# Attention times v in tiles of 128 rows by 32 columns, the row sums right behind it, and a copy split over two engines

## The chip, the cores and the metric

The kernel runs on one core of a Trainium2 chip. The metric is the device time of one execution in microseconds (us); the kernel before takes 552.08 us, the median of three runs (551.88 to 552.08). Of the core's engines the text names TensorE (PE in the profile's rows, PEld for its weight loads), VectorE (DVE), ScalarE (ACT), GpSimd (POOL) and SyncE (SP), whose queue issues nearly all DMAs. TensorE writes into PSUM, which here is used as four pairs of banks, PS[0] to PS[3].

## The reference

Three layers follow each other, on 4 batches of 576 positions: attention with rotated q and k, 8 heads of 64 channels; a gated layer with a layer norm and a product over positions; a layer with a short convolution as gate. The change lies in the first:

```python
q_rot, k_rot = rotate(q), rotate(k)
scores = (1 / sqrt(D)) * q_rot @ k_rot^T          # 576 x 576 for each head
scores = scores - max(scores, axis=-1)
attn = exp(scores)
attn = attn / (sum(attn, axis=-1) + 1e-09)
out = attn @ v                                    # then the two other layers
```

All arithmetic is fp32 in its accuracy: products with q and k are made of high and low parts in a reduced format, the product with v and the row sums are fp32 matmuls. An fp32 matmul shows as two MATMUL instructions with a weight load each.

## The kernel before, in words

Heads are taken in pairs: 16 pairs, two heads side by side in the 128 partitions. For each pair the loop in `attention` (L805 to 824) calls `phase`, which puts two things on TensorE in a fixed, hand-written order of units: the exponent scores of pair i (nine units `t` and `T`, L662 and L670, each followed by an exponential on ScalarE, L675, that leaves keys on partitions and query positions on columns in nine tiles `e`) and the plain scores of pair i + 1 (`y`, `x` and `S`, L610 and L620), of which VectorE takes row maxima out of PSUM (L613, L622), because the exponential needs each row's maximum ahead. For the pairs 1 to 14 the order begins `y t y t t x t ...`; in the last phase there are no maxima. Which pair of banks each unit takes follows from a small model of when the banks come free: in the phases after the first, the first `y` takes PS[0], the first `t` PS[1], the second `y` PS[2], the second `t` PS[3], and the third `t` takes PS[0] again, which it may write when the first maximum is done.

Behind each phase stands what the text calls the product stage. `pv_unit` (L689 on) multiplies the exponentials with v: four units of two key blocks each, for 512 of the 576 keys, into PS[3]: the weights are 64 channels of v for 128 keys, the moving data 288 query positions, and the two halves of the positions go to the partitions 0 to 63 and 64 to 127 (L699). Two such matmuls stand beside each other in the array. A fifth call with `(8,)` adds the remaining 64 keys of both heads with tiles of 64 rows by 64 columns (L709) and copies PS[3] to the tile `xu` on ScalarE (L713, through the helper at L263), from where two DMAs on SP's queue store it (L717). Then `sum_unit` (L722 on) adds the exponentials over the keys by matmuls with ones: tiles of 128 rows by 32 columns, four beside each other, into PS[2] (L733). ScalarE copies the sums (`ss`, L737), a DMA spreads them (`rc`), VectorE takes reciprocals in `sum_end` (L745), and a DMA stores these.

GpSimd has added a part of the exponentials before (tiles `ac`), and in six of the pairs it adds more, so that the sums take 24 MATMULs instead of 32.

During the product stage VectorE and ScalarE prepare pair i + 2: four elementwise operations that rotate q and k (`prep_high`, L259), casts on ScalarE (`qp`, `qh`, `kh`), and, in the pairs 1 to 8, the conversion of a weight tile (`wa_half`, L309 to L315); in the pairs 9 to 13 VectorE makes the low part of k instead (`kl`).

The order of the instructions on each engine is set once by a planner (`Plan.order`). Every operation is added with a cost in us. TensorE's operations keep the order in which they are added; on the other engines, whenever an engine is free in the planner's own time, the operation that is ready and has the earliest due time goes next, where due times are counted back from the end along the dependences (an engine may also be held for a more urgent operation that comes soon). The costs decide only this order; on the chip each engine runs its list and waits on semaphores.

Of the kernel before, what the change touches and what calls it, by code (L numbers as in the profile page):

```python
# [21 lines left out]
B, HP, S, DM, HALF = 4, 4, 576, 512, 288  # L22
# [120 lines left out]
def dve(n):  # L143
    return 0.08 + n / 960
# [20 lines left out]
FP32 = 0.48  # L165
# [5 lines left out]
def mixer_kernel(ctx: ExitStack, tc: tile.TileContext, qk, v, vrem, cs, w_in, g_ln, w_sgT, b_sg,  # L171
                 w_out, w_val, conv_w, w_out2, out):
    nc = tc.nc
# [3 lines left out]
    add = P.add  # L177
# [14 lines left out]
    xu_d = [dram.tile([HP, 128, S], F32, name=f"xu_d{b}") for b in range(B)]  # L192
# [69 lines left out]
    def acopy(out_, in_, n, r, w, after=()):  # L262
        return add("Act", act(n), lambda: nc.scalar.copy(out_(), in_()), r, w, after)  # L263
# [384 lines left out]
    EU = {}  # L648
# [40 lines left out]
    def pv_unit(i, us):  # L689

        j2 = i % 2
        pv, kp = PS[3], ("ps", 3)
        if us[0] < 8:
            j = UNITS[us[0]][0]

            def mm():
                for h in range(2):
                    for hf in range(2):
                        nc.tensor.matmul(pv[64 * hf:64 * hf + 64, h, 0:HALF], VM[j2][:, j, h], E[EU[i, us[hf]]][:, h],  # L699
                                         start=j == 0, stop=False, skip_group_check=True)  # L700
            add("PE", 2 * FP32 + (0.2 if not j else 0.0), mm, [*[("e", EU[i, u]) for u in us], ("vm", j2)], [kp])
            return
        e = E[EU[i, 8]]

        def mm():
            for hf in range(2):
                for h in range(2):
                    rows = slice(64 * h, 64 * h + 64)
                    nc.tensor.matmul(pv[64 * hf:64 * hf + 64, h, 0:HALF], VR[j2][rows], e[rows, hf], start=False, stop=True,  # L709
                                     skip_group_check=True)  # L710
        add("PE", FP32 + 0.1, mm, [("e", EU[i, 8]), ("vr", j2)], [kp])
        xu = XU[j2]
        acopy(lambda: xu, lambda: pv[:, :, 0:HALF], S, [kp], [("xu", j2)])  # L713

        def st(q):
            for hf in range(2):
                q.dma_start(out=xu_d[i // HP][i % HP, :, HALF * hf:HALF * hf + HALF].rearrange("(h d) c -> d h c", h=2),  # L717
                            in_=xu[64 * hf:64 * hf + 64])
        dma(290, st, [("xu", j2)], [("xu_d", i)], n=2)

    def sum_unit(i, ps, kps):

        j2 = i % 2
        src = [(ones, ones, [(E[EU[i, u + hf]], h) for h in range(2) for hf in range(2)], ("e", EU[i, u]),
                ("e", EU[i, u + 1])) for u in (4, 6)[adds(i) // 2 - 1:]]
        src.append((ones, ones, [(AC[hf], h) for h in range(2) for hf in range(2)], ("ac", 0), ("ac", 1)))
        e = EU[i, 8]
        src.append((*ones_b, [(E[e], hf) for h in range(2) for hf in range(2)], ("e", e)))

        def mm():  # L730
            for n, x in enumerate(src):
                for t, (a, y) in enumerate(x[2]):
                    nc.tensor.matmul(ps[32 * t:32 * t + 32, 0, 0:HALF], x[t // 2], a[:, y], start=n == 0,  # L733
                                     stop=n == len(src) - 1, skip_group_check=True)
        add("PE", len(src) * FP32 + 0.15, mm, [*[k for x in src for k in x[3:]], ("consts",)], [kps])
        ss, rc = SS[0], RC[j2]
        add("Act", act(HALF), lambda: nc.scalar.activation(ss, ps[:, 0, 0:HALF], AF.Copy, bias=1e-9), [kps], [("ss", 0)])  # L737

        def rows(q):
            q.dma_start(out=rc, in_=ss[0:97:32].rearrange("t (p c) -> t p c", c=9))  # L740
        dma(5, rows, [("ss", 0)], [("rc", j2)])
# [22 lines left out]
    def attention():  # L764
        keep_busy(16)
        first_pairs()

        def phase(i, vl):

            order = "ytyttxtttyttyxTS" if i + 1 < NPAIR else "ttttttttT"  # L770
            if not i:
                order = "xtttyttytyttyxTS"
            free = [0.0, 0.0, 0.74 if i else 0.0, 0.0]
            pe, ac, dv = 0.2, 0.0, 0.0
            nt, xs, ys = 0, iter(range(2)), iter(range(2, 6))
            for x, what in enumerate(order):
                ks = range(4) if x < len(order) - 4 else range(3)
                at_once = [k for k in ks if free[k] <= pe]
                k = max(at_once, key=lambda k: free[k]) if at_once else min(ks, key=lambda k: free[k])
                pe = max(pe, free[k])  # L780
                if what in "tT":
                    pe += 4 * PASS if what == "t" else 8 * PASS + 0.24
                    act_at = max(ac, pe + 0.22)
                    ac, free[k] = act_at + 0.55, act_at + 0.75
                    st_unit(i, nt, PS[k], ("ps", k))
                    add_unit(i, nt)
                    nt += 1
                else:
                    pe += 2 * PASS if what == "S" else MAXIMA[what == "y"][0]
                    dve_at = max(dv, pe + 0.29)  # L790
                    dv = dve_at + (0.67 if what == "S" else MAXIMA[what == "y"][1])
                    free[k] = dv + 0.15
                    s_unit(i + 1, {"x": xs, "y": ys, "S": iter((8,))}[what].__next__(), PS[k], ("ps", k))
                if not x:
                    first = [P.last_pe, *vl]
                    if 2 <= i + 1 < NPAIR:
                        prep_low(i + 1, first)
                if x == (12 if i < FOUR else 0):
                    job_s(i, [P.last_pe])
            if i + 1 < NPAIR:  # L800
                s_end(i + 1)

        vl = []
        for i in range(NPAIR):
            if i + 2 < NPAIR:  # L805
                prep_load(i + 2)
            if i and i + 1 < NPAIR:
                load_v(i + 1)
            if i:
                job_loads(i)  # L810
            phase(i, vl)
            ep.append(P.last_pe)
            rot = [P.last_pe]
            if 0 < i < FOUR or i == NPAIR - 1:
                sum_end(i - 1, [*rot, *P.writer.get(("mn", (i + 1) % 2, 1), ())] if i + 1 < NPAIR else ())
            if i + 2 < NPAIR:
                rot = prep_high(i + 2, [P.last_pe, *P.writer[("mn", (i + 1) % 2, 1)]])
            vl = job_v(i, [P.last_pe], rot)
            if FOUR <= i < NPAIR - 1:
                sum_end(i - 1, P.writer["kl", (i + 1) % 3])  # L820
            for us in ((0, 2), (1, 3), (4, 5), (6, 7), (8,)):
                pv_unit(i, us)
            sum_unit(i, PS[2], ("ps", 2))
        sum_end(NPAIR - 1)

    def unit(cost, mm, r, new=True):
# [414 lines left out]
```

## Time and profile before

| | |
|---|---|
| median of three runs | 552.08 us |
| the profiled execution | 552.56 us, its span 550.8 us |
| TensorE, its weight loads | 541.4 us busy (98%), 463.3 (84%) |
| VectorE | 411.7 us busy (75%) |
| ScalarE | 278.4 us busy (51%) |
| GpSimd | 247.5 us busy (45%) |
| granted TensorE clock | 0.998 of full speed |

The span runs from the first instruction to the last. Busy times are from a trace of one execution; matmuls are pipelined, so that one that is shown with 0.41 us can be followed by the next after much less, and their ends are modelled. The chain of work that ended last is followed back from the last instruction, at each step to what released it. Idle time of an engine that nothing waits for costs nothing.

### The profile page before, as it was taken

What the parts mean: (1) busy time and instruction counts of PE and PEld (TensorE: products, weight loads), DVE (VectorE), ACT (ScalarE), POOL (GpSimd) and SP (SyncE); (2) the same over time, 40 slices, a digit from 0 to 9 for tenths busy, and PEclk for the clock granted to TensorE, in tenths of its full rate; (3) what the DMA queues carried; (4) which work ended last, traced back from release to release, by engine and by line L of the source; (5) the groups of instructions that cost most, each with busy time, mean ns of one, the idle gap of its engine ahead of it and who ended that gap; (6) DMA issues with size and microseconds to landing.
All of it is one profiled execution on the core that took longest, in us unless ns stands there. A gap on an engine that the chain in (4) does not pass through costs nothing.

```text
span 550.8 us, 11758 instructions
## 1 busy us (share of the span) xinstructions
PE 541.4 (98%) x4592; PEld 463.3 (84%) x4592; DVE 411.7 (75%) x595; ACT 278.4 (51%) x451; POOL 247.5 (45%) x229
## 2 busy tenths in 40 slices
PE   6999999999999999999999999999999999999996
PEld 5877777777777777679989989989999998899985
DVE  7878888888888888969768556654979997649610
ACT  3567766776666667635526136134157543334221
POOL 5545555555555555456967677554610011222000
PEclk9999999999999999999999999999999999999999
DMA  5565656565666664774484762643264211110022
GB/s 187 141 195 142 184 152 175 160 185 153 188 171 160 168 198 103 214 223 111 131 295 119 231 189 75 196 142 124 104 208 128 73 44 72 44 58 1 0 77 96
DMA packets 58024, 77.39 MB, mean 141 GB/s; under 512 B 29392, under 2 KB 34000, under 8 KB 57968
## 3 DMA queue, kind: packets, MB, share of 16 engines
q1 hardware_dynamic: 57664, 76.37, 46.8%
q8 instruction: 36, 0.59, 0.4%
q10 hardware_dynamic: 304, 0.26, 0.1%
q14 instruction: 20, 0.16, 0.1%
HBM read 55.94 MB, written 18.95 MB: 136 GB/s over the span
## 4 chain that ended last, share of the span: by engine, by line
PE 96%; DVE 2%; DMA 1%; ACT 0%; issue 0%; SPq 0%; ACTq 0%; DVEq 0%
PE ps L840 55%; PE ps L662 12%; PE ps L699 12%; PE ps L733 6%; PE ps L670 4%; PE ps L610 4%; PE ps L709 2%; PE ps L951 2%; DVE raw L259 1%; DVE mx L613 1%; DMA raw<-qk 1%; PE ps L620 1%; DVE mn L622 0%; ACT ob L263 0%; ACT kh L263 0%
## 5 line engine op out<-in xcount | busy, mean ns | idle before, releaser
L613 DVE TENSOR_REDUCE mx<-ps 128x2 f32<-128x640 f32 (+1 forms) x96 | 89.1, 957 | 28.8 <-PE ps L610 21.9
L675 ACT ACTIVATE e<-ps 128x576 f32<-128x576 f32 x144 | 87.0, 652 | 20.3 <-PE ps L670 10.9
L699 PE MATMUL ps<-e,vm 128*64 128x288 f32 x512 | 65.6, 409 | 0.0
L699 PEld LDWEIGHTS ps<-e,vm 128*64 128x64 f32 x512 | 35.3, 137 | 24.7 <-issue 2.6
L260 POOL TENSOR_TENSOR ac<-e,e 128x576 f32<-128x576 f32 x32 | 45.2, 1431 | 9.4 <-ACT e L675 9.4
L840 PE MATMUL ps<-s_h,vn 128*128 128x288 f32 x256 | 46.9, 295 | 0.0
L259 DVE TENSOR_TENSOR raw<-raw,cst 128x1152 f32<-128x1152 f32 (+1 forms) x33 | 42.0, 1272 | 0.5 <-DMA raw<-qk 0.5
L263 ACT CAST qp<-raw 128x512 fp32r<-128x512 f32 x16 | 18.6, 1164 | 45.2 <-DVE raw L259 45.2
L840 PEld LDWEIGHTS ps<-s_h,vn 128*128 128x128 f32 x256 | 38.3, 188 | 0.0
L662 PE MATMUL ps<-qh,kh 64*128 64x288 f32 x256 | 38.3, 295 | 0.0
L662 PE MATMUL ps<-qh,kl 64*128 64x288 f32 x256 | 37.9, 292 | 0.0
L662 PE MATMUL ps<-ql,kh 64*128 64x288 f32 x256 | 37.8, 292 | 0.0
L662 PE MATMUL ps<-mr,one_r 64*128 64x288 f32 x256 | 37.7, 290 | 0.0
L260 POOL TENSOR_TENSOR vs<-vs,u 128x576 f32<-128x576 f32 x16 | 27.0, 1688 | 19.3 <-DVE vs L955 16.8
L610 PE MATMUL ps<-kh,qp 64*128 64x320 f32 (+1 forms) x256 | 32.7, 312 | 2.3 <-ACT kh L263 2.2
L1032 DVE SCALAR_TENSOR_TENSOR gt<-xm,cw,gt 128x576 f32<-128x576 f32 x32 | 28.9, 909 | 1.8 <-ACT gt L1029 1.4
L610 PEld LDWEIGHTS ps<-kh,qp 64*128 64x128 f32 x256 | 21.7, 184 | 10.0 <-ACT kh L263 7.7
L309 DVE TENSOR_SCALAR wt<-wt 128x256 f32<-128x256 f32 (+1 forms) x28 | 16.4, 586 | 16.5 <-ACT wt L319 16.5
L260 POOL TENSOR_TENSOR xl<-xs,xh 128x576 fp32r<-128x576 f32 x2 | 5.3, 2633 | 50.0 <-ACT xh L263 50.0
L840 PE MATMUL ps<-XL,w_h 128*128 128x288 f32 x128 | 27.4, 296 | 0.0
L840 PE MATMUL ps<-XH,w_l 128*128 128x288 f32 x128 | 27.4, 295 | 0.0
L840 PE MATMUL ps<-XH,w_h 128*128 128x288 f32 x128 | 27.4, 295 | 0.0
(181 smaller groups left out, 1493.4 us busy)
## 6 DMA issues: line engine op xcount, KB each, us to landing
raw<-qk SPq DMA_DIRECT2D x31, 576.0 KB
xu_d<-xu SPq DMA_DIRECT2D x32, 144.0 KB
rb<-r_d SPq DMA_DIRECT2D x32, 144.0 KB
xs<-xu_d SPq DMA_DIRECT2D x16, 288.0 KB
x_d<-xs SPq DMA_DIRECT2D x16, 288.0 KB
g_d<-vs SPq DMA_DIRECT2D x16, 288.0 KB
vm<-v SPq DMA_DIRECT2D x16, 256.0 KB
wr<-w_in SPq DMA_DIRECT2D x8, 512.0 KB
```

Of the source, the lines that this page charges most:

```text
L259: return add("DVE", dve(n), lambda: nc.vector.tensor_tensor(out_(), a(), b(), op), r, w, after, lock=True)
L260: return add("Pool", pool(n), lambda: nc.gpsimd.tensor_tensor(out_(), a(), b(), op), r, w, after, lock=True)
L263: return add("Act", act(n), lambda: nc.scalar.copy(out_(), in_()), r, w, after)
L610: nc.tensor.matmul(ps[:, h, w * y:w * y + w], QP[j2][rows, c], kh[rows, keys], start=True, stop=True)
L613: add("DVE", MAXIMA[n // 2 > 0][1], lambda: nc.vector.tensor_reduce(out=MX[j2][:, n // 2 > 0, :, chunks[0]:chunks[-1] + 1], in_=ps[:, :, 0 ...
L662: nc.tensor.matmul(ps[:, h, 0:HALF], x[rows, keys] if o < 3 else x[rows], y[rows, cols], start=o == 0, stop=o == 3)
L670: nc.tensor.matmul(ps[:, hf, 0:HALF], x, y[:, cols], start=o == 0, stop=o == 3)
L675: add("Act", 0.62, lambda: nc.scalar.activation(E[n], ps[:, :, 0:HALF], AF.Exp), [kps], [("e", n)])
L699: nc.tensor.matmul(pv[64 * hf:64 * hf + 64, h, 0:HALF], VM[j2][:, j, h], E[EU[i, us[hf]]][:, h], start=j == 0, stop=False, skip_group_chec ...
L733: nc.tensor.matmul(ps[32 * t:32 * t + 32, 0, 0:HALF], x[t // 2], a[:, y], start=n == 0, stop=n == len(src) - 1, skip_group_check=True)
L840: nc.tensor.matmul(out_(y), lhs(p, k, y), rhs(q, k, y), start=not z, stop=ends and z == len(terms) - 1)
L1032: add("DVE", dve(S) + 0.05, lambda dd=dd, m=m, x2=x2, gt=gt: nc.vector.scalar_tensor_tensor(gt(), x2()[:, m:m + S], cw[:, 5 * dd + m:5 * d ...
```

## The change

In `pv_unit` each product of two key blocks is cut into four tiles of 128 rows by 32 columns instead of two of 128 by 64: the tile `t` takes 32 of the 64 channels (`t % 2`) for one half of the positions (`t // 2`), so there are twice as many matmuls and weight loads of half the width. In `attention` the row sums are issued behind the four units of the product, and the remainder `(8,)` last. The copy of PS[3], which follows the remainder, is split: head 0 on ScalarE, head 1 on VectorE, each 128x288 elements, and the two stores wait for both. Some of the planner's costs change with it.

```diff
             def mm():
                 for h in range(2):
-                    for hf in range(2):
-                        nc.tensor.matmul(pv[64 * hf:64 * hf + 64, h, 0:HALF], VM[j2][:, j, h], E[EU[i, us[hf]]][:, h],
-                                         start=j == 0, stop=False, skip_group_check=True)
-            add("PE", 2 * FP32 + (0.2 if not j else 0.0), mm, [*[("e", EU[i, u]) for u in us], ("vm", j2)], [kp])
+                    for t in range(4):
+                        nc.tensor.matmul(pv[32 * t:32 * t + 32, h, 0:HALF], VM[j2][:, j, h, 32 * (t % 2):32 * (t % 2) + 32],
+                                         E[EU[i, us[t // 2]]][:, h], start=j == 0, stop=False, skip_group_check=True)
+            add("PE", 2 * FP32 + (0.1 if not j else 0.0), mm, [*[("e", EU[i, u]) for u in us], ("vm", j2)], [kp])
             return
...
-        acopy(lambda: xu, lambda: pv[:, :, 0:HALF], S, [kp], [("xu", j2)])
+        acopy(lambda: xu[:, 0], lambda: pv[:, 0, 0:HALF], HALF, [kp], [("xu", j2, 0)])
+        add("DVE", dve(HALF), lambda: nc.vector.tensor_copy(xu[:, 1], pv[:, 1, 0:HALF]), [kp], [("xu", j2, 1)])
...
-        dma(290, st, [("xu", j2)], [("xu_d", i)], n=2)
+        dma(290, st, [("xu", j2, h) for h in range(2)], [("xu_d", i)], n=2)
...
-        add("PE", len(src) * FP32 + 0.15, mm, [*[k for x in src for k in x[3:]], ("consts",)], [kps])
+        add("PE", len(src) * FP32, mm, [*[k for x in src for k in x[3:]], ("consts",)], [kps])
...
-            for us in ((0, 2), (1, 3), (4, 5), (6, 7), (8,)):
+            for us in ((0, 2), (1, 3), (4, 5), (6, 7)):
                 pv_unit(i, us)
             sum_unit(i, PS[2], ("ps", 2))
+            pv_unit(i, (8,))
```

## Rows read from the trace of the kernel before

**Rows 1.** The page: busy us of each engine, and the chain by engine.

```profile
PE 541.4 (98%) x4592; PEld 463.3 (84%) x4592; DVE 411.7 (75%) x595; ACT 278.4 (51%) x451; POOL 247.5 (45%) x229
...
PE 96%; DVE 2%; DMA 1%; ACT 0%; issue 0%; SPq 0%; ACTq 0%; DVEq 0%
```

**Rows 2.** Stretches (start:end): length, busy us by engine, clock, DMA share, GB/s.

```profile
26.00:236.50 210.50, 210.37 (x2438) 152.18 (x2437) 179.96 (x250) 142.32 (x233) 109.40 (x93) 1.00 0.61 170
236.50:546.00 309.50, 309.50 (x1939) 292.56 (x1936) 211.28 (x320) 122.84 (x200) 122.76 (x95) 1.00 0.38 118
```

**Rows 3.** Chain, pair 7: start us, us, engine, tile, line, instructions.

```profile
122.98 4.03 PE ps L699 x32
127.01 0.65 PE ps L709 x8
127.66 2.08 PE ps L733 x32
```

**Rows 4.** Chain, pair 9, where the sums are shorter.

```profile
155.33 1.59 PE ps L733 x24
```

**Rows 5.** TensorE's timeline, pair 7: start, us, line, out<-in, shapes; first row cut at 125.0.

```profile
122.91 2.40 PE L699 MATMUL ps<-e,vm 128*64 128x288 f32 x18
...
122.91 4.10 PE L699 MATMUL ps<-e,vm 128*64 128x288 f32 x32
126.94 0.71 PE L709 MATMUL ps<-e,vr 64*64 64x288 f32 x8
...
129.67 0.41 PE L610 MATMUL ps<-kh,qp 64*128 64x320 f32 x2
```

**Rows 6.** ScalarE's timeline, pair 7, the copy and the cast behind it.

```profile
127.91 0.63 ACT L263 COPY xu<-ps 128x576 f32<-128x576 f32 x1
128.45 0.67 ACT L263 CAST kh<-raw 128x576 fp32r<-128x576 f32 x1
```

**Rows 7.** Timeline, pair 14: the remainder and the copy that follows it.

```profile
221.70 0.72 PE L709 MATMUL ps<-e,vr 64*64 64x288 f32 x8
...
222.48 0.64 ACT L263 COPY xu<-ps 128x576 f32<-128x576 f32 x1 [0.85 <-DMA krl<-kl]
```

**Rows 8.** VectorE's timeline at the end of pair 7's product stage; in brackets its idle time.

```profile
129.32 0.43 DVE L315 SCALAR_TENSOR_TENSOR wf<-wr,wt 128x256 int32<-128x256 int32 x1
129.66 0.21 DVE L745 RECIPROCAL rc<-rc 128x9 f32<-128x9 f32 x1
130.12 0.83 DVE L613 TENSOR_REDUCE mx<-ps 128x2 f32<-128x640 f32 x1 [0.25 <-PE ps L610]
```

**Rows 9.** TensorE's weight loads, first of the third exponent unit behind pair 7.

```profile
131.00 0.19 PEld L662 LDWEIGHTS ps<-qh,kh 64*128 64x128 f32 x2
```

**Rows 10.** Timeline, pair 13: a maximum, and a weight load that waited for it.

```profile
202.75 0.83 DVE L613 TENSOR_REDUCE mx<-ps 128x2 f32<-128x640 f32 x1 [0.80 <-PE ps L610]
...
203.63 0.19 PEld L620 LDWEIGHTS ps<-kh,qr 128*128 128x128 f32 x1
```

**Rows 11.** VectorE by line and form: busy us, mean ns; the rows of 288 elements.

```profile
L259 DVE TENSOR_TENSOR raw<-raw 128x288 f32<-128x288 f32 x4 | 1.8, 458 | 0.1
```

**Rows 12.** VectorE's timeline at the end of pair 8's product stage.

```profile
143.21 0.42 DVE L315 SCALAR_TENSOR_TENSOR wf<-wr,wt 128x256 int32<-128x256 int32 x1
143.96 1.58 DVE L613 TENSOR_REDUCE mx<-ps 128x2 f32<-128x640 f32 x2 [0.32 <-PE ps L610]
```

**Rows 13.** VectorE's timeline, pair 11, and where TensorE starts the next scores.

```profile
181.88 0.76 DVE L259 TENSOR_TENSOR raw<-raw 128x576 f32<-128x576 f32 x1
...
183.23 0.21 DVE L745 RECIPROCAL rc<-rc 128x9 f32<-128x9 f32 x1
184.00 0.83 DVE L613 TENSOR_REDUCE mx<-ps 128x2 f32<-128x640 f32 x1 [0.56 <-PE ps L610]
...
183.54 0.42 PE L610 MATMUL ps<-kh,qp 64*128 64x320 f32 x2
```

**Rows 14.** SP's queue, pair 7: the stores of the copy.

```profile
134.07 2.22 SPq L717 DMA_DIRECT2D xu_d<-xu  x2
```

## The prediction

> **What bounds the kernel now.** I read the page first: TensorE is busy 98% of the span and holds 96% of the chain that ended last [rows 1], where VectorE has 2%. The view of stretches says the same of attention (26.0 to 236.5 us) and of all that follows: 210.4 of 210.5 us and 309.5 of 309.5 us, at full clock [rows 2]. The whole change lies in attention, and behind it TensorE never idles; so each microsecond that TensorE's order loses or gains there moves the end by as much, and what another engine does counts only where it makes TensorE wait. The order on TensorE is the order of the program: the scores and exponentials of a pair of heads, then a product stage, and so 16 times.
>
> The chain shows that stage in its parts: 4.03 us for the 32 matmuls with v, 0.65 for the 8 of the remainder, 2.08 for the 32 of the row sums, 6.75 together [rows 3]; in six of the pairs the sums are only 24 matmuls, 1.59 us [rows 4]. The timeline gives the pace inside: from 18 to 32 matmuls with v the end moves by 4.10 - 2.40 = 1.70 us, seven groups of two, 0.243 us a group [rows 5]. The sums go in groups of four tiles of 32 columns, and eight fewer of them save 2.08 - 1.59 = 0.49 us, again 0.243 to 0.245 a group. So a group of four narrow tiles costs what two wide ones do, and each part pays something for the entry into and the exit from its tile shape: 4.03 - 16 x 0.243 = 0.14 us for the product with v, 0.65 - 2 x 0.243 = 0.16 for the remainder, 2.08 - 8 x 0.243 = 0.14 for the sums.
>
> **Part 1: tiles of 32 columns, sums right behind, remainder last.** 64 matmuls in 16 groups of four, then the 8 groups of the sums in the same shape, one entry and one exit: 24 x 0.243 + 0.14 = 5.97, and 0.65 for the remainder: 6.62 instead of 6.75 (6.13 instead of 6.27 where the sums are shorter). One shape change of 0.14 us goes, 16 x 0.14 = 2.2 us. The entry from the full array into narrow tiles is not in the trace (before, they are entered from the remainder). The two other changes bound it: if the new entry costs up to 0.03 more the sum is 1.8, if it costs less it is 2.4; I take 2.2, the sums' own row. The 512 added matmuls and weight loads I cost at nothing: loads run beside matmuls, 152 of the 210 us of attention against 210 of matmuls [rows 2], and the sums keep 0.243 with as many loads.
>
> The Trainium skill speaks against this part: by "TensorEngine Tiling (Array Packing)", section Instruction Overhead, each matmul carries about 60 cycles of its own, so one should not buy tiles with more instructions; 512 x 60 cycles at 2.4 GHz are 12.8 us, an estimate from that page alone. It is a rival below.
>
> **Part 2: the copy moves behind the stage's end and half of it goes to VectorE.** The old copy, 0.63 us on ScalarE, stood between the casts of q and k, 1.8 us ahead of the next scores [rows 5, 6]. Now the accumulator (the fourth pair of banks) is complete only with the remainder's last matmul. In an undisturbed place (at 222 us) the copy began 0.06 us after the remainder's modelled end [rows 7], and that end, 126.94 + 0.71, lies 0.06 behind the stage's end. So both halves can start 0.12 us after the next scores have begun.
>
> ScalarE is free there: the copy of the sums, done earlier now, is out of the way, and the next exponential needs a finished unit of new scores first. VectorE is not. Call R the start of its first maximum (L613) of the next scores before the change, 0.45 us into them (130.12 to 129.67) [rows 5, 8]. TensorE waits on this instruction without slack: the third unit of exponent scores reuses its banks, and its first weight load started at 131.00, while the maximum ended at 130.95 [rows 8, 9]; VectorE's end reaches TensorE's load 0.05 us later (203.58 to 203.63) [rows 10]. So whatever delays the first maximum delays TensorE by the same, and it isn't made up for.
>
> Price of the half copy: no row has it. The nearest is the addition of 128x288 elements, 0.458 us [rows 11]; from above the maximum over 640 elements out of PSUM, 0.83 [rows 10]; from below the reciprocal of 9, 0.21 [rows 8]. An independent successor starts some 0.08 before such an end (129.66 after 129.32 + 0.43) [rows 8]. I take 0.458 - 0.08 = 0.38 us, the row of the same width; the ends are 0.13 and 0.75. VectorE keeps its order, so the first maximum stands behind the copy: the copy can begin first, and its banks are needed first, by the second unit of exponent scores.
>
> New times, all by R; with 0.14 saved the scores start at R - 0.59, the copy can start at R - 0.47, the maximum's matmuls are ready at R - 0.14:
> - Pairs 1, 3, 5, 7: weight conversions and a reciprocal hold VectorE till 129.66 + 0.13 = R - 0.33 [rows 8]. The maximum starts at R - 0.33 + 0.38 = R + 0.05.
> - Pairs 2, 4, 6, 8: the reciprocal is earlier; L315 starts at 143.21 and frees VectorE 0.34 later, R - 0.41 [rows 12]. The maximum: R - 0.03.
> - Pairs 0 and 9 to 13: VectorE is free by R - 0.64 (183.23 + 0.13 against 184.00) [rows 13]. The maximum: R - 0.47 + 0.38 = R - 0.09.
> - Pairs 14 and 15: no maxima follow, and the fourth bank pair is wanted late: the full 0.14.
>
> Sum: 4 x 0.05 - 4 x 0.03 - 6 x 0.09 - 2 x 0.14 = -0.74 us. So of 2.2 us some 1.5 is given back as waits for L613.
>
> The rows thus put 0.38 us on the engine that TensorE waits for next; the 0.63 us of the whole copy on ScalarE would touch no maximum. By the Trainium skill, "TensorEngine Tiling (Array Packing)", section PSUM Bottleneck, ScalarE and VectorE should share the evacuation; by that rule alone the split is free and the sum -2.2.
>
> What else moves: in pairs 9 to 12 the cast of k, freed of the copy ahead of it, follows the addition's end at 182.64 and ends 0.03 + 0.67 later, at 183.34, 0.06 ahead of the new start at 183.54 - 0.14 = 183.40 [rows 6, 13]: just hidden; if not, it costs what it ends later, some 0.05 in four pairs. The stores of the copy went out at 134.07, 5.5 us after the copy's end [rows 6, 14]; 1.8 us later they still find it done, and on SP's queue behind them wait weight loads for later pairs; the copy of the sums and its reciprocal chain come 0.8 us earlier. Without that cover a later transfer would slip by 1.8 us, none of it read for the next two pairs.
>
> Forecast: the profiled execution took 552.56 us (span 550.8 and 1.8 around it), so 551.8 for it; it stands 0.5 above the median of the three runs, 552.08, for which I say 551.3.
>
> **Rivals.**
> - The copy is hidden, full gain. If it occupies VectorE for 0.13 us as the reciprocal does, the maximum is ready at R - 0.20 or earlier and R - 0.14 rules: 552.1 - 2.2 = 549.8. For it: VectorE idles 0.25 to 0.56 us just there [rows 8, 12, 13]. Against: the four rows of 288 elements take 0.458 [rows 11].
> - Slower: VectorE's queue at the start of the scores. The order on it is planned with costs below the rows (0.35 us for L315, whose row has 0.43 [rows 8]), so one more operation may come between the stage's end and the first maximum. Another conversion there (0.34) in eight pairs costs 2.7: 551.3 + 2.7 = 554.0. Gain and loss balance where the maximum is ready 0.16 us late by its own matmuls, as a mean over 14 pairs (2.2 / 14); the forecast has 1.5 / 14 = 0.11; from 0.24 it is slower by over 0.2%. Against: the planner gives the copy and the maximum earlier due times than conversions.
> - The change doesn't do what it says: the exit price of the wide tiles turns up at the entry of the narrow ones or of the scores. Then only the loss is left: 552.1 + 1.5 = 553.6. Against: the parts' extras are alike (0.14, 0.16, 0.14) whatever comes before and after.
> - An added matmul pays its own slot. Matmuls and loads of the sums go at 0.243 / 8 = 0.03 us each; 512 x 0.03 = 15 us, 567. Against: the sums keep 0.243 a group with the same eight instructions.
>
> **How the numbers follow.** Forecast 0.50, with its own range 550.8 to 551.9; full gain 0.20; slower by VectorE's queue 0.13; no gain from the shapes 0.08; own slots 0.02; the rest (0.07) for a new order elsewhere, to either side. 0.2%, 1.1 us, is about what a measurement of this kernel can tell from no change: faster means below 551.0, slower above 553.2. Faster: the full gain, the lower tenth of the forecast's and part of the rest, 0.34. Slower: most of the queue's and of the lost gain, 0.16. Same: 0.50. The range 549.7 to 553.6 takes in the full gain and the lost gain; the upper price of the copy, 0.75 (0.37 more in 14 pairs, 5.2 us, 556.5), stays out with most of the queue's.
>
> **What would show it.** Right: product with v and sums in one piece of about 5.97 us (5.5 with short sums), the remainder 0.65 behind it; a VectorE copy of some 0.46 us ahead of the first L613; the gap from the start of the scores to the first maximum 0.50 to 0.65 us instead of 0.45; the third unit's first load later than 1.33 us into the scores by the same. Wrong: that gap still 0.45 (then the full gain), the maximum ahead of the copy, groups slower than 0.243 us, or a different extra where the shape changes.

## The result, and the profile after

The changed kernel took 555.25 us in the median of four runs (554.31 to 555.75) against 552.08 before; the ratio is 1.0056, 95% interval 1.0038 to 1.0073. I had said 551.3 (549.7 to 553.6): the change is slower where I had forecast no change, and outside the range. The profiled execution is the fastest of the four, 554.31 us with a span of 552.5; a second one, taken with the experiments, took 555.48 with a span of 553.69.

The page of the changed kernel, busy time and the chain by engine:

```profile
PE 542.4 (98%) x5104; PEld 461.5 (84%) x5104; DVE 415.8 (75%) x611; ACT 277.3 (50%) x451; POOL 245.7 (44%) x229
...
PE 82%; DVE 8%; DMA 4%; ACT 3%; issue 2%; SPq 0%; ACTq 0%; DVEq 0%
```

The view of its stretches, from the first product stage to the end of attention and from there to the end:

```profile
25.50:238.24 212.74, 211.17 (x2950) 150.29 (x2949) 182.75 (x264) 141.13 (x232) 107.91 (x93) 1.00 0.60 166
238.24:548.00 309.76, 309.76 (x1940) 292.58 (x1936) 213.18 (x322) 122.94 (x199) 121.81 (x96) 1.00 0.37 119
```

In [rows 1] TensorE held 96% of the chain that ended last; now it holds 82%, and VectorE, ScalarE and DMAs have pieces of it. In [rows 2] TensorE was idle for 0.13 us of attention; now it is for 1.57 of 212.74. (The busy time hides more: matmuls that are followed late are shown longer.) Most of the time is lost in attention, by waits.

TensorE's timeline in pair 7 of the changed kernel, in start, us, line, out<-in and shapes:

```profile
123.64 4.09 PE L699 MATMUL ps<-e,vm 128*32 128x288 f32 x64
127.55 1.15 PE L734 MATMUL ps<-e,ones 128*32 128x288 f32 x16
...
129.60 0.72 PE L709 MATMUL ps<-e,vr 64*64 64x288 f32 x8
130.25 0.42 PE L610 MATMUL ps<-kh,qp 64*128 64x320 f32 x2
```

Product and sums run as one piece, 129.60 - 123.64 = 5.96 us, the remainder takes 0.65, and the stage 6.60 in place of 6.75 [rows 3, 5]. The gain of the tiles is there. What follows it in the same pair is not as forecast. ScalarE, VectorE and TensorE's weight loads, the same kernel, start of the next scores (130.25):

```profile
129.79 0.41 ACT L738 ACTIVATE ss<-ps 128x288 f32<-128x288 f32 x1
130.93 0.40 ACT L263 COPY xu<-ps 128x288 f32<-128x288 f32 x1 [0.73 <-DVE xu L714]
...
130.03 0.43 DVE L315 SCALAR_TENSOR_TENSOR wf<-wr,wt 128x256 int32<-128x256 int32 x1
130.38 0.21 DVE L746 RECIPROCAL rc<-rc 128x9 f32<-128x9 f32 x1
130.50 0.40 DVE L714 COPY xu<-ps 128x288 f32<-128x288 f32 x1
130.81 1.55 DVE L613 TENSOR_REDUCE mx<-ps 128x2 f32<-128x640 f32 x2
...
131.38 0.19 PEld L662 LDWEIGHTS ps<-qh,kh 64*128 64x128 f32 x2 [0.29 <-ACT xu L263]
...
131.89 0.19 PEld L662 LDWEIGHTS ps<-qh,kh 64*128 64x128 f32 x2
```

VectorE copies its half at 130.50 and starts the first maximum 0.56 us into the scores, where it was 0.45 [rows 8]: that is my forecast. But ScalarE begins its half only when VectorE's is done (the bracket: idle for 0.73 us, released by VectorE's `xu`), 0.68 into the scores. PS[3] comes free at 1.08, and the second exponent unit loads its first weights at 131.38, 1.13 in, after a wait for ScalarE's `xu`. The third unit follows 1.64 in; in [rows 9] it was 1.33.

Two other places lose time. The first is pairs 9 and 11. GpSimd's timeline at the product stage of pair 9, then VectorE's, in the kernel before:

```profile
156.69 0.17 POOL L267 COPY mark<-kl 1x1 f32<-1x1 f32 x1 [5.10 <-DVE kl L259]
156.83 0.79 POOL L260 TENSOR_TENSOR s_l<-xs,s_h 128x288 fp32r<-128x288 f32 x1
...
151.75 1.35 DVE L259 TENSOR_TENSOR raw<-raw,cst 128x1152 f32<-128x1152 f32 x1
```

and the same in the changed kernel:

```profile
152.60 0.82 POOL L260 TENSOR_TENSOR s_l<-xs,s_h 128x288 fp32r<-128x288 f32 x1
...
152.82 1.82 DVE L259 TENSOR_TENSOR raw<-raw,cst 128x1152 f32<-128x1152 f32 x1
```

The planner has put GpSimd's subtraction (`s_l`) 5 us earlier in the stage, beside VectorE's first multiply, which takes 1.82 us instead of 1.35. In pair 11 it is another subtraction (`w_l`, 0.73 us), and the multiply takes 1.72. Over all fourteen traces (before, after, e1 to e12) ten such multiplies run beside a GpSimd subtraction for 0.42 to 0.61 us; they take 1.64 to 1.82 us, each longer than 1.35 by its overlap less 0.13. The 396 others, none beside GpSimd for more than 0.12 us, take 1.29 to 1.36. All that hangs on the multiply (the rotation, the cast of k, the next scores) comes as much later, and ScalarE, by the same new plan, copies the sums ahead of that cast. The stage takes 6.68 us where pairs 10 and 12 have 6.12 and 6.13.

The second is behind the last pair. VectorE, SP's queue, GpSimd and TensorE's weight loads in the second profile of the changed kernel, whose attention ended at 238.44:

```profile
241.89 0.29 DVE L311 TENSOR_SCALAR wt<-wt 128x256 int32<-128x256 int32 x1
242.10 0.45 DVE L714 COPY xu<-ps 128x288 f32<-128x288 f32 x1
...
240.25 0.62 SPq L741 DMA_DIRECT2D rc<-ss  x1
242.58 1.28 SPq L718 DMA_DIRECT2D xu_d<-xu  x2
243.96 0.55 SPq L849 DMA_DIRECT2D xs<-xu_d  x1
244.55 0.45 SPq L322 DMA_DIRECT2D wr<-w_in  x1
...
254.55 1.27 POOL L260 TENSOR_TENSOR w_l<-wf,w_h 128x512 fp32r<-128x512 f32 x1 [5.16 <-ACT w_h L263]
...
255.87 0.30 PEld L842 LDWEIGHTS ps<-XH,w_l 128*128 128x128 f32 x2 [0.79 <-POOL w_l L260]
```

and SP's queue and GpSimd in the kernel before, whose attention ended at 236.48:

```profile
236.60 1.27 SPq L717 DMA_DIRECT2D xu_d<-xu  x2
239.29 0.43 SPq L322 DMA_DIRECT2D wr<-w_in  x1
...
250.79 1.29 POOL L260 TENSOR_TENSOR w_l<-wf,w_h 128x512 fp32r<-128x512 f32 x1 [3.33 <-ACT w_h L263]
```

VectorE's half of pair 15 stands in its queue behind weight conversions (one of them, beside a GpSimd subtraction, takes 1.47 us where it takes 0.43 alone) and ends at 242.55. The store goes out 6.0 us later than before, and the load of the next weights, behind it on SP's queue, 5.3 us later (counted from the end of attention, 4.0 and 3.3). The low part of these weights, `w_l`, is ready at 255.82, and TensorE, which wants it at 255.1, waits. In the first profile the same chain was 1.2 to 1.6 us earlier (load at 242.98) and nothing waited. That is the 1 us by which the two profiles differ behind attention; the other runs have no trace.

The lengths below are worked out from the starts of TensorE's matmuls: the product stage of pairs 0 to 8 (before: 6.75), the same of pair 9, the median of the 14 stretches of scores, the stretch from the first product stage to the end of attention, and from there to the end of the span. Each ratio is over all runs, to runs of the kernel before taken beside them (medians 552.06 to 552.13); it is not the quotient of the medians, least so in e2 and e7, whose runs are spread.

```
kernel                  stage  pair 9  scores  attention  behind it  time    ratio [95%]
before                  6.754  6.27    7.08    210.50     314.29     552.08
changed                 6.603  6.68    7.41    212.72     314.26     555.25  1.0056 [1.0038, 1.0073]
e1  changed again       6.603  6.68    7.41    212.75     315.25     555.17  1.0056 [1.0044, 1.0069]
e2  halves parallel     6.603  6.68    7.18    210.02     318.01     553.31  1.0035 [1.0017, 1.0052]
e3  one copy, ScalarE   6.604  6.14    7.10    208.74     315.76     551.70  0.9994 [0.9985, 1.0003]
e4  planner's table     6.607  6.45    7.39    213.57     314.27     554.96  1.0052 [1.0039, 1.0064]
e5  narrow tiles only   6.741  6.26    7.09    210.70     314.26     552.04  1.0001 [0.9993, 1.0010]
e6  one copy, order     6.603  6.15    7.10    209.03     314.28     550.85  0.9974 [0.9963, 0.9984]
    of before kept
e7  cast of k first     6.603  6.59    7.41    212.47     314.89     555.43  1.0076 [1.0055, 1.0098]
e8  split, old place    6.754  6.27    7.16    211.06     314.27     552.71  1.0009 [1.0000, 1.0017]
e9  split, order kept   6.603  6.13    7.54    214.49     314.56     556.41  1.0076 [1.0064, 1.0088]
e10 e9, parallel        6.603  6.14    7.18    209.28     315.99     551.84  0.9992 [0.9982, 1.0001]
e11 remainder last only 6.754  6.27    7.11    210.66     314.28     552.21  1.0003 [0.9995, 1.0012]
e12 last two pairs old  6.603  6.68    7.41    212.99     314.26     554.83  1.0052 [1.0037, 1.0066]
```

The span of the second profile is 2.92 us longer than before, and that divides so: start 0.30 less; the product stages of pairs 0 to 14 but 9 and 11, 2.12 less (0.2 of it a stall that the kernel before had in pair 13); the stages of pairs 9 and 11 0.82 more; 12 stretches of scores 3.72 more (the two behind pairs 9 and 11 are unchanged, since their late start hides the copies); the last pair 0.17 less; behind attention 0.96 more.

### The profile page after: what moved, and what is told of

It is laid out like the page before. It is cut to its first block, busy times and chain, and to the rows that moved or that the text cites. A ratio compares the mean times of both kernels' runs of the same rounds, so it can differ in the third digit from the quotient of the medians.

```text
span 552.5 us, 12851 instructions
## 1 busy us (share of the span) xinstructions
PE 542.4 (98%) x5104; PEld 461.5 (84%) x5104; DVE 415.8 (75%) x611; ACT 277.3 (50%) x451; POOL 245.7 (44%) x229
## 4 chain that ended last, share of the span: by engine, by line
PE 82%; DVE 8%; DMA 4%; ACT 3%; issue 2%; SPq 0%; ACTq 0%; DVEq 0%
PE ps L842 55%; PE ps L662 10%; PE ps L699 7%; DVE raw L259 4%; DMA raw<-qk 3%; PE ps L734 3%; DVE mx L613 2%; PE ps L670 2%; ACT e L675 2%; PE ps L610 2%; PE ps L953 2%; PE ps L709 1%; ACT xu L263 1%; DMA wr<-w_in 1%; DVE xu L714 0%
## 5 line engine op out<-in xcount | busy, mean ns | idle before, releaser
L613 DVE TENSOR_REDUCE mx<-ps 128x2 f32<-128x640 f32 (+1 forms) x96 | 88.7, 954 | 24.9 <-PE ps L610 17.5
L699 PE MATMUL ps<-e,vm 128*32 128x288 f32 x1024 | 65.4, 408 | 0.0
L699 PEld LDWEIGHTS ps<-e,vm 128*32 128x32 f32 x1024 | 31.6, 110 | 27.8 <-issue 2.6
L662 PEld LDWEIGHTS ps<-qh,kh 64*128 64x128 f32 x256 | 24.0, 184 | 4.3 <-ACT xu L263 3.5
L842 PE MATMUL ps<-s_l,vn 128*128 128x288 f32 x128 | 27.3, 294 | 0.0
```

The source lines that it names most:

```text
L613: add("DVE", MAXIMA[n // 2 > 0][1], lambda: nc.vector.tensor_reduce(out=MX[j2][:, n // 2 > 0, :, chunks[0]:chunks[-1] + 1], in_=ps[:, :, 0 ...
L662: nc.tensor.matmul(ps[:, h, 0:HALF], x[rows, keys] if o < 3 else x[rows], y[rows, cols], start=o == 0, stop=o == 3)
L699: nc.tensor.matmul(pv[32 * t:32 * t + 32, h, 0:HALF], VM[j2][:, j, h, 32 * (t % 2):32 * (t % 2) + 32], E[EU[i, us[t // 2]]][:, h], start=j ...
L842: nc.tensor.matmul(out_(y), lhs(p, k, y), rhs(q, k, y), start=not z, stop=ends and z == len(terms) - 1)
```

## Experiments

Theory A: the two halves run one after the other, and the second exponent unit waits for PS[3]. Rival B, my own forecast's term: VectorE's half delays the first maximum, and that is the cost. C: in pairs 9 and 11 the loss is ScalarE's new order, the sums ahead of the cast of k; its rival: VectorE's longer multiply. (The expectation of e3 calls another rival C.) D: what saves time is one change of tile shape fewer.

**e1, the changed kernel again** (no edit).

> The changed kernel once more, for its spread and a second profile. Expected: 554.3 to 555.8 us, 1.005 of before; in the attention's phases the second exponent unit again starts about 1.13 us after the end of the product stage, and in pairs 9 and 11 the next scores again start 0.56 us late. If the about 1 us by which its other runs lie above the profiled one is a phase wait that comes and goes, the second profile shows it in other pairs.

555.17 us; the waits in the scores are the same to 0.02 us. The variable part is behind attention (315.25 against 314.26), not in the phases as I had guessed.

**e2, the halves in parallel.** Each half reads a bank of its own; the kernel's dependences are kept per tile, and PS[3] is one tile. The edit takes back the dependence between the two readers; the next writer of PS[3] still waits for both.

```diff
-        acopy(lambda: xu[:, 0], lambda: pv[:, 0, 0:HALF], HALF, [kp], [("xu", j2, 0)])
-        add("DVE", dve(HALF), lambda: nc.vector.tensor_copy(xu[:, 1], pv[:, 1, 0:HALF]), [kp], [("xu", j2, 1)])
+        both = []
+        def half(h):
+            both.append((nc.vector.tensor_copy if h else nc.scalar.copy)(xu[:, h], pv[:, h, 0:HALF]))
+            if len(both) == 2:
+                tc.declare_no_dep(both[1].ins, both[0].ins, reason="two readers of two banks")
+        add("Act", act(HALF), lambda: half(0), [kp], [("xu", j2, 0)])
+        add("DVE", dve(HALF), lambda: half(1), [kp], [("xu", j2, 1)])
```

> The changed kernel with one thing else: the two half copies of PS[3] no longer wait for each other (they read two banks). Every engine's order is the same. Theory A (the halves ran one after the other, so PS[3] came free at 1.09 us after the product stage and not at 0.65, and the second exponent unit waits for it): both halves start 0.2 after the product, the unit starts at 0.93 again, 12 phases win back about 0.33 us each: 555.25 - 4.0 = 551.2 us (550.7 to 551.8), ratio about 0.999. Rival B (my prediction's term: VectorE's half delays the first reduction and that costs): VectorE does the same work at the same place, so 555 us as the change, ratio 1.005.

ScalarE, VectorE and the weight loads in pair 7, scores from 128.78:

```profile
128.92 0.40 ACT L716 COPY xu<-ps 128x288 f32<-128x288 f32 x1 [0.19 <-PE ps L709]
...
129.04 0.40 DVE L716 COPY xu<-ps 128x288 f32<-128x288 f32 x1
129.36 1.55 DVE L613 TENSOR_REDUCE mx<-ps 128x2 f32<-128x640 f32 x2
...
129.56 0.21 PEld L662 LDWEIGHTS ps<-qh,kh 64*128 64x128 f32 x2
...
130.23 0.18 PEld L662 LDWEIGHTS ps<-qh,kh 64*128 64x128 f32 x2
```

Both halves take 0.40 us side by side; PS[3] is free at 0.66, the second unit loads at 0.78 (129.56) without a wait, and the scores fall from 7.41 to 7.18. What remains is B: the first maximum at 0.58 and the third unit's load at 1.45 (130.23) in place of 1.33. So A costs 0.23 us a stretch and B 0.08 to 0.10; 12 stretches: 2.7 and 1.0. The Trainium skill ("PSUM — Partial Sum Buffer", section PSUM bank collisions raise a hardware error) says that two engines may not read one bank and quadrant at once, but may read different banks; the two lengths of 0.40 agree with the second half, and no run here shows the first. The time, 553.31 (551.98 to 556.74), is neither A's 551.2 nor B's 555: attention, 0.48 us shorter than before, promises 551.6. The profiled run took 555.48, and its view of stretches shows where it lost that; the other runs have no trace:

```profile
252.00:256.00 4.00, 2.15 (x11) 1.92 (x12) 3.45 (x12) 1.46 (x3) 2.69 (x4) 0.90 0.83 220
256.00:260.00 4.00, 4.00 (x24) 4.00 (x23) 3.17 (x6) 3.13 (x6) 3.67 (x5) 0.68 0.07 15
260.00:264.00 4.00, 4.00 (x33) 4.00 (x33) 3.86 (x7) 1.68 (x3) 2.56 (x3) 1.00 0.00 0
```

Attention ends 2.8 us earlier than in e1, but GpSimd starts on `w_l` only 1.2 us earlier (253.31 against 254.55); TensorE's weight loads wait for `w_h` (1.5 us) and `w_l` (0.8), and the granted clock is 0.68 in the 4 us that follow: part of them at the lower of the two levels, 1.2 GHz.

**e3, the whole copy on ScalarE.**

```diff
-        acopy(lambda: xu[:, 0], lambda: pv[:, 0, 0:HALF], HALF, [kp], [("xu", j2, 0)])
-        add("DVE", dve(HALF), lambda: nc.vector.tensor_copy(xu[:, 1], pv[:, 1, 0:HALF]), [kp], [("xu", j2, 1)])
+        acopy(lambda: xu, lambda: pv[:, :, 0:HALF], S, [kp], [("xu", j2, h) for h in range(2)])
```

> The changed kernel with the whole copy (128x576) on ScalarE alone, so the new tiles and the remainder last without the split. Theory A: the copy takes 0.63 us from about 0.2 after the product stage, PS[3] is free at 0.83, the second exponent unit's turn is at 0.93: no wait left, and ScalarE's order at pairs 9 and 11 is that of before: 555.25 - 4.0 - 1.1 = 550.1 us (549.5 to 551), ratio 0.9965. Rival C (a single copy behind the product is too late as well, the unit waits up to 0.1 to 0.2 us in each phase): 551.7 to 553.

Pair 7, scores from 128.37:

```profile
128.51 0.64 ACT L263 COPY xu<-ps 128x576 f32<-128x576 f32 x1 [0.18 <-PE ps L709]
...
128.83 1.58 DVE L613 TENSOR_REDUCE mx<-ps 128x2 f32<-128x640 f32 x2
...
129.20 0.19 PEld L662 LDWEIGHTS ps<-qh,kh 64*128 64x128 f32 x2
...
129.71 0.19 PEld L662 LDWEIGHTS ps<-qh,kh 64*128 64x128 f32 x2
```

One copy of 0.64 us ends 0.78 into the scores, and the second unit loads at 0.83; first maximum and third unit are where they were before (0.46 and 1.34). The scores are 7.10 but for two stretches of 7.47, behind pairs 6 and 12, whose cause I have not found. Attention is 1.8 us shorter than before. The time is not (551.70): 1.5 us are lost behind attention, where TensorE waits 0.9 us for GpSimd (`t`) and 0.4 for ScalarE (`gl`).

**e4, the planner's table of the banks.**

```diff
-            free = [0.0, 0.0, 0.74 if i else 0.0, 0.0]
+            free = [0.0, 0.0, 0.1 if i else 0.0, 1.1 if i else 0.0]
```

> The changed kernel with the planner's table of when the banks come free set to where the change puts them (bank pair 2 at 0.1, bank pair 3 at 1.1 us): the second exponent unit takes another bank pair, and the two halves stay one after the other. Theory A: the late release of PS[3] is hidden, 555.25 - 4.0 - 1.1 (ScalarE's order at pairs 9 and 11 also goes back) = 550.1 us (549.5 to 551). Rival B (VectorE's half and its queue cost by themselves): 554 us, only the 1.1 of pairs 9 and 11 comes back.

A miss, and it decides nothing between A and B: in pair 7 the second exponent unit still waits for ScalarE's `xu`, since four units come in a row and there are four pairs of banks. In pairs 9 to 13 the first unit, now in PS[2], waited for the copy of the sums (stage 6.45).

**e5, the narrow tiles alone**, in the kernel before: L699 as in the change, all else as it was.

> The kernel before with the product's tiles alone changed: 128 rows by 32 columns, 64 matmuls in place of 32; the remainder stays ahead of the sums, the copy is whole and on ScalarE. The product stage then has as many changes of tile shape as before (128x32, 64x64, 128x32). Theory D (a change of shape costs some 0.15 us, a narrower tile and the doubled number of matmuls nothing): 552.1 us, ratio 0.9995 to 1.0005, product stage 6.75 us. Rival (each added matmul has a cost that only the saved change of shape hid): the stage is longer by up to 32 x 10 ns = 0.3 us, 16 pairs: up to 557 us, ratio above 1.002.

Stage 6.741, 552.04 us. 64 matmuls of 32 columns take what 32 of 64 columns took (the 10 ns a matmul of the rival were a guess, from no row); TensorE's timeline, pair 7 of e5, against [rows 5]:

```profile
122.25 4.09 PE L699 MATMUL ps<-e,vm 128*32 128x288 f32 x64
126.27 0.72 PE L709 MATMUL ps<-e,vr 64*64 64x288 f32 x8
```

**e6, one copy, order of before kept.** As e3, but pairs 14 and 15 in the old form, with the old costs for the planner.

```diff
+            late = i < 14
-            for us in ((0, 2), (1, 3), (4, 5), (6, 7)):
+            for us in ((0, 2), (1, 3), (4, 5), (6, 7), *[(8,)][late:]):
                 pv_unit(i, us)
             sum_unit(i, PS[2], ("ps", 2))
-            pv_unit(i, (8,))
+            if late:
+                pv_unit(i, (8,))
```

> As the whole copy on ScalarE alone with the new tiles and the remainder last, but pairs 14 and 15 keep the order of before (remainder ahead of the sums) and the planner's costs of before, so that the order of every engine after the attention is that of the kernel before. Theory (the attention gains about 1.6 to 2.3 us without the split, and the run with one copy lost 1.5 us of it after the attention, where the planner had put the work on the weights in another order): attention ends at 234.6 to 235, the time is 550.3 to 550.8 us, ratio 0.997. Rival (the stage after the attention is bound by the weights' own chain, whatever the order; before had 0.9 us of room there): the time is 551.3 us or more, and TensorE waits in the first stage after the attention for the low parts of the weights.

550.85 us, ratio 0.9974 (0.9963 to 0.9984): the one version that beats both kernels. Behind attention it loses nothing (314.28), and its runs lie within 0.65 us. It still has the two stretches of 7.4. In them VectorE's third maximum starts 2.86 to 2.88 us into the scores, in place of 2.51 in the pairs just before, though its matmuls start where they did; why is open.

**e7, the cast of k first in pairs 9 and 11.**

```diff
-        add("Act", act(HALF), lambda: nc.scalar.activation(ss, ...), [kps], [("ss", 0)])
+        add("Act", act(HALF), lambda: nc.scalar.activation(ss, ...), [kps], [("ss", 0)],
+            P.writer["kh", (i + 2) % 3] if i in (9, 11) else ())
```

> The changed kernel with one order else: in pairs 9 and 11 ScalarE casts the next keys ahead of the copy of the row sums, as in all other pairs; nothing else is moved. Theory C: the next scores start on time there (2 x 0.56 us won), but then the two phases have the late PS[3] as the others (2 x 0.33 lost again): 555.2 - 0.45 = 554.7 us, ratio 1.0045 to 1.0055. Rival (the order costs nothing, VectorE's longer first multiply by itself is what is late): 555.2 us and the scores after pairs 9 and 11 still 0.5 late.

C falls, its rival holds: with the cast first the stages are still 6.59 and 6.54, since VectorE's multiply still takes 1.82 us beside GpSimd (1.75 in pair 11). ScalarE's order was worth 0.1 us of the 0.5. The time does not show it: 555.43 (554.69 to 558.54), with two of the six runs at 557.91 and 558.54, which have no trace.

**e8, the split alone, at its old place** in the kernel before (the copy's two lines as in the change).

> The kernel before with the split of the copy alone, at its old place: the remainder still ahead of the sums, so that 2 us of sums lie over the two halves. Theory A (the halves run one after the other, but that costs only behind the product): PS[3] is free before the next scores' second unit, no wait for it; VectorE's half delays the first reduction by at most 0.1 us in pairs 1 to 8: 552.1 to 552.9 us. Rival (the split costs wherever it stands, by VectorE's queue): the first reduction late by 0.1 and more in all 14 pairs and the third bank wait with it: 553.4 us or more.

552.71: PS[3] is not waited for, the sums lie over both halves; VectorE's half adds 0.07 us to the scores behind pairs 1 to 8 (7.166 against 7.092, means of eight).

**e9, the split with the order of before**, and **e10, the same in parallel.** As e6, with the split in pairs 0 to 13; e10 adds e2's edit.

```diff
+        if i < 14:
             acopy(lambda: xu[:, 0], lambda: pv[:, 0, 0:HALF], HALF, [kp], [("xu", j2, 0)])
-            add("DVE", dve(HALF), lambda: ...
+            add("DVE", 0.0, lambda: ...
+        else:
+            acopy(lambda: xu, lambda: pv[:, :, 0:HALF], S, [kp], [("xu", j2, h) for h in range(2)])
```

> The changed kernel with the order of all other work as before: the split copy in pairs 0 to 13 is costed at 0 for the planner, pairs 14 and 15 keep the order and the whole copy of before, so GpSimd's order is that of before in all pairs and VectorE's differs by the 14 half copies alone. Theory (of what the change lost, the halves one after the other cost 0.32 us in each scores stretch; GpSimd's split moved under VectorE's first multiply cost 0.5 in pairs 9 and 11; the weights' chain after the attention 0 to 1): all 14 scores stretches at 7.41 us, product stage 6.60 and 6.13 without the two of 6.68, nothing lost after the attention: 554.3 us (554 to 554.6), ratio 1.004. Rival (the planner's order is no part of it): 555.2 us, ratio 1.0056, stages of 6.68 us at pairs 9 and 11.

> As the run with the pinned order, and the two half copies free to run side by side; every engine's order is the same as there. Theory: what is left is VectorE's half ahead of the first reduction, 0.10 us a scores stretch (7.185 in place of 7.41), 14 times 0.22 won: 554.3 - 3.1 = 551.2 us (551 to 551.7), ratio 0.998 to 0.999: the change as my prediction took it. Rival: the two copies slow each other or the time is lost after the attention, 552 us or more.

e9 took 2 us more than expected, for a reason that its trace shows (pair 7, scores from 131.23):

```profile
131.37 0.40 ACT L263 COPY xu<-ps 128x288 f32<-128x288 f32 x1 [0.18 <-PE ps L709]
...
131.80 0.46 DVE L715 COPY xu<-ps 128x288 f32<-128x288 f32 x1 [0.22 <-ACT xu L263]
132.18 1.55 DVE L613 TENSOR_REDUCE mx<-ps 128x2 f32<-128x640 f32 x2
...
132.31 0.19 PEld L662 LDWEIGHTS ps<-qh,kh 64*128 64x128 f32 x2 [0.24 <-DVE xu L715]
```

With a cost of 0 the planner issued ScalarE's half first, so now VectorE waits, with the first maximum behind it (0.95 into the scores instead of 0.56): 7.54 us. The same order without the dependence (e10) has 7.18. So one wait is worth 0.36 us a stretch this way round and 0.23 the other. GpSimd's order is that of before here, and pairs 9 and 11 have stages of 6.13: that part of the theory holds. e10 took 551.84 (550.67 to 553.21), 0.5 above what I forecast for the change and 0.1 above its own range. Its profiled run (552.31) lost 1.7 us behind attention waiting for weights, though the last two pairs are in the old form: their load was issued 5.2 us after the end of attention, in e6 3.4 and in the kernel before 2.8. Why it was later is open.

**e11, the remainder last alone**: the kernel before with the order of the change in pairs 0 to 13, tiles of 64 columns, whole copy.

> The kernel before with the remainder alone moved behind the sums (pairs 0 to 13, tiles of 64 columns kept, whole copy on ScalarE). Theory D (the saving is one change of tile shape, which needs both the narrow tiles and the new place): stages 6.75 as before, since 128x64, 128x32, 64x64 are as many changes, and the scores stretch 7.10 in place of 7.08: 552.1 to 552.4 us, ratio 1.000 to 1.0006. Rival (the place of the remainder saves it): stage 6.60, 550.8 us, ratio 0.9975.

Stage 6.754, 552.21: D holds. The place by itself saves nothing and the tiles 0.01 us (e5); together they save one change of shape, 0.14 to 0.15 us.

**e12, only the last two pairs old**: the change, with e6's edit and the whole copy in pairs 14 and 15.

> The changed kernel with pairs 14 and 15 alone in the old form (remainder ahead of the sums, whole copy on ScalarE, the planner's costs of before there); pairs 0 to 13 as in the change, VectorE's half first, GpSimd's split still under VectorE's multiply in pairs 9 and 11. Theory (in the change the copy of pair 15 comes 4 to 5 us later, its store holds SP's queue, the load of the next weights behind it is issued at 243 to 244.6 in place of 239.3, and TensorE waits 0 to 0.9 us for those weights after the attention): the load is issued by 241, no wait for the weights' low parts, the stretch from the end of the attention to the end of the program is 314.3 us as before, runs within 0.6 us of each other, 554.2 to 554.6 us, ratio 1.004. Rival (what comes late after the attention has another cause): 555.2 us, runs over 1 us apart, the wait for the low parts still there in some.

554.83 (554.47 to 555.07), 0.2 above what I expected. SP's queue and GpSimd:

```profile
239.18 1.27 SPq L721 DMA_DIRECT2D xu_d<-xu  x2
...
241.88 0.42 SPq L322 DMA_DIRECT2D wr<-w_in  x1
...
253.40 1.29 POOL L260 TENSOR_TENSOR w_l<-wf,w_h 128x512 fp32r<-128x512 f32 x1 [3.00 <-ACT w_h L263]
```

The store is 3.4 us earlier than in e1, the load behind it 2.7; `w_l` is ready in time, and the stretch behind attention is 314.26. My "by 241" for the load was not met. The first profile of the changed kernel had 314.26 too, so that this single profile proves little; the runs speak for it: they lie within 0.6 us, the nine of the changed kernel within 1.44.

## Why the prediction was wrong

- **The shapes: right.** 24 groups in one piece 5.96 us (5.97 said), the remainder 0.65, 0.15 us less a stage (0.14 said). The rule that each matmul carries some 60 cycles of its own (the Trainium skill, "TensorEngine Tiling (Array Packing)", section Instruction Overhead) does not show as added time here, where the tiles lie side by side: e5 doubles the matmuls of the product, and the stage takes 6.74 against 6.75. The rivals "own slots" and "no gain from the shapes" fall.
- **The price of VectorE's half: nearly right.** Said: the first maximum 0.50 to 0.65 us into the scores; measured 0.55 to 0.58. Said: 1.5 us given back in 14 stretches; e2 has 1.0 in 12. One copy touches no maximum (e3): 7.10 us against 7.18. So the rule of the Trainium skill ("TensorEngine Tiling (Array Packing)", section PSUM Bottleneck) to use both ScalarE and VectorE, taken alone, has no support here.
- **The step that failed: "So both halves can start 0.12 us after the next scores have begun."** VectorE's began 0.25 us in, behind the reciprocal in its queue, but ScalarE's only at 0.68, when VectorE's was done. I had asked what each engine was busy with, and not what orders two readers of one tile. PS[3] came free at 1.08 us instead of 0.66 (e2), and the second exponent unit, by which "its banks are needed first", as I had written, waited: 2.7 us in 12 stretches. The binding wait was PS[3], not L613. e2 and e10 show it by taking the one dependence away.
- **A moved step in a planned program moves others.** I gave "a new order elsewhere" 7 in 100 and no mechanism. In pairs 9 and 11 the new order cost 0.8 us against before, 1.1 against the stages they would otherwise have had: 0.2 of it by ScalarE's order (e7), the rest by GpSimd's subtractions under VectorE's multiplies. In e9 GpSimd's order is that of before and VectorE's has only the copies more, and the stages are short; the subtractions were not moved by themselves, but the length of every multiply follows its overlap with them.
- **"Without that cover a later transfer would slip by 1.8 us, none of it read for the next two pairs."** In pairs 0 to 13 no wait of that kind shows. Behind pair 15 there is no next pair: the load of weights on the same queue slipped by 5.3 us in the second profile, where TensorE's weight load waited 0.8 us for what is made of it; in the first it waited for nothing.

By these steps the change loses 2.7 + 1.0 + 0.8 + 1.0 and wins 2.1 and 0.2: 3.2 us in the second profile, whose span is 2.92 longer since it starts 0.30 earlier. The medians differ by 3.17. My rival "slower by VectorE's queue" came within 1.3 us of the time (554.0), but by luck, through another mechanism: in no pair did a further conversion come between.

## What to carry to other kernels

Before a copy is split over two engines, look whether the two readers can run at once: two banks do not help if the dependence is kept for the tile that holds both, and then the split ends later than one copy (0.40 + 0.40 and a handover against 0.64). Of a step that is moved to the end of a stage, follow the last repetition as well as the usual one, with everything behind it on its queue. Where a planner orders the other engines, compare their orders before and after the edit, engine by engine; of this change's loss 1.8 us (second profile) came from work that it did not touch.

## What the runs showed of the hardware

- A multiply of 128x1152 on VectorE took 1.82 us in place of 1.35 where GpSimd's subtraction (0.82 us, begun 0.22 earlier) ran beside it. The Trainium skill ("SBUF — State Buffer", section Who interferes with whom) says that a VectorE instruction with two SBUF inputs contends with a GpSimd instruction that reads SBUF, and that the ports they share are an exclusive lock. By the rows a full block would be 0.60 us, and 0.47 was lost; in all ten such multiplies of these traces the loss is the overlap less 0.13, so they agree but for that 0.13 (spans on GpSimd are rough).
- ScalarE and VectorE read two banks of PSUM side by side at 0.40 us each (e2), no slower than one after the other in the changed kernel.
- In e2, after waits of 1.5 and 0.8 us of the weight loads in the first stage behind attention, the granted clock was 0.90 and then 0.68 in stretches of 4 us; the stretch from the end of attention to the end was 3.7 us longer than before, 1.4 more than the waits.
- A change of tile shape costs 0.14 to 0.15 us here: product stages in three orders with the same number of changes took 6.741 to 6.754 us (before, e5, e11), that with one fewer 6.603. No single change was measured by itself.
